# From the fourth chunk on, x is convolved raw in float32 by eight array tiles, and output rows are scaled on GpSimd

## The chip, the cores and the metric

The kernel runs on one core of one Trainium2 chip. The metric is the device time of one launch in microseconds (us): 1162.91 us, the median of three runs from 1162.69 to 1163.97. TensorE is called PE in the profile, VectorE DVE, ScalarE ACT, GpSimd POOL; SP only issues DMAs here. A weight load of PE has rows of its own (PEld).

## The reference

An input x of 8 sequences of 4160 rows and 192 columns is convolved along the sequence: eight heads of 24 columns, seven taps per head, causal (six zero rows ahead of each sequence). The taps are a softmax of a weight table. The result goes, row by row, through a layer with a nonlinearity:

```python
out = np.einsum('hk,bskhg->bshg', w, x_unf)        # convolution: y
...
h = x @ w_in                                       # 192 -> 1024
e = np.exp(h - h_max)
sm = e / (np.sum(e, axis=-1, keepdims=True) + 1e-09)
solu = h * sm
ln = (solu - mu) / np.sqrt(var + 1e-06) * g_ln
return (ln @ w_out).astype(np.float32)             # 1024 -> 192
```

All in float32. The 33280 rows are 260 tiles of 128.

## The kernel before

**Halves.** To use float16 matmuls at float32's accuracy, operands are split: an upper float16 half and a lower one that holds the rest. `y` is written as halves (`upper` on ACT, L313; `lower` on DVE, L322), turned by DMA so that columns lie on partitions (`yT`, and `y2`, a copy of a part on the other 64 partitions), and multiplied with the halves of `w_in` (`whi`, `wlo`).

**One tile of 128 rows.** PE adds up `ph`, 128x1024: `emit_rows` (L736, eight matmuls of 512 columns) and two matmuls with the lower half on 64 array rows (`emit_third`, L759), which are issued in turns for the two halves of the array. DVE scales `ph` and takes its extremum (`emit_max`, L790), ACT makes the exponential (`emit_exp`, L797), DVE multiplies it with `ph` (`emit_mul`, L807), ACT writes the upper half (L815) and the square sums (L819), POOL writes the lower half (`emit_lo`, L827) and SP issues its DMA transpose into `pT`. Five tiles later PE multiplies `pT` with `w_out`'s halves (`emit_out`, L859) into `po`, and DVE empties it into `raw` (`emit_evac`, L869). `raw`'s rows wait until a group of eight tiles has its roots; then each is scaled (`row`, L936 on ACT and L940 on DVE in turns) and stored.

**Three tiles are one step** (`three_steps`), and the order of every engine is written out by hand there. On PE: rows of tile a, a place for convolution, the thirds of a, b and c, rows of b, `po` of an older tile, a second place for convolution, rows of c, two more `po`. `ph` has three pairs of PSUM banks. The two banks left are called singles: `po`, convolution products and small totals take them in turns.

**Chunks.** x is convolved chunk by chunk, one chunk ahead of its use: one chunk of 1024 rows, one of 1056, then 2080 each, 17 in all. A window is 128 rows on partitions, 16 of them overlap, so that it gives 112 rows of `y`. A matmul of `taps` (128 x 112, a band) with windows gives 112 rows of one head. The first three chunks are taken as they are, in float32 (`exact`). From the fourth on, POOL makes halves of x (`halve_steps`, L236, L240, L243), and a head of 9 or 10 windows costs three float16 matmuls (`taps_hi` with `xh`, `taps_hi` with `xl`, `taps_lo` with `xh`); two heads make a group, six matmuls into one single. A chunk has eight groups.

**Scale.** Before a chunk is convolved its magnitude is needed: `sum_squares` takes peaks of quarter pieces on DVE (L181), a small matmul (L95) adds them over the partitions, and a chain of tiny instructions gives the scale `s`.

**What sets the time of such work.** `chores` says at which tile of a chunk its successor's convolutions, turns, copies, loads and peaks are issued; `Queue` lets POOL's halves in piece by piece. Where 2080 rows don't fill tiles, `open` copies up to 96 columns from the chunk before (L339, L340) and mixes two scales (L346, L347).

Of the kernel before, what the change touches and what calls it, by code (L numbers as in the profile page):

```python
# [13 lines left out]
ALU = mybir.AluOpType  # L14
# [5 lines left out]
def kernel(  # L20
# [30 lines left out]

# [9 lines left out]
    spans = []  # L61
    for b in range(B):
        cuts = [0, S // 2, S] if b else [0, FIRST, S // 2, S]
        spans += [(b, t, z - t) for t, z in zip(cuts, cuts[1:])]
    NCH = len(spans)
    NWM = max(-(-n // CW) for _, _, n in spans)
# [55 lines left out]

    class Chunk:
        def __init__(self, ch):
# [7 lines left out]
            self.y16 = {}  # L132
            self.raw = [None] * self.np
            self.sums, self.scaled = 0, False
            self.exact = ch < 3
            self.peaks = 2 * self.np if ch < 2 else self.np if ch < 4 else 0
            self.part = None

        def load(self, j):
# [3 lines left out]
            t = xp.tile(  # L143
                [P, PW, D], F32, name=f"xr_{self.ch}_{j}", tag="xr", bufs=XR
            )
# [67 lines left out]
        def square_peaks(self):  # L213

            if self.peaks < 2 * self.np:
                q = self.part[:, self.peaks : 2 * self.np]
                act.activation(q, q, AF.Square, scale=16.0)

        def add_up(self, bank=None):
            self.tp = total(self.part[:, 0 : 2 * self.np], f"x{self.ch}", bank)  # L220

        def halve_steps(self, j, quick=False):

            if j == 0:
                both = xp.tile([P, 2, NWM, D], F16, name=f"xs_{self.ch}", tag="xs", bufs=2)
                self.xh, self.xl = both[:, 0], both[:, 1]
            a, z = self.cuts[j], self.cuts[j + 1]
            r, h = self.raw[j][:, 0 : z - a, :], self.xh[:, a:z, :]
            xl = self.xl[:, a:z, :]
            size = (z - a) * D * 1e-3  # L230

            def upper():
                if quick:
                    act.activation(h, r, AF.Copy, scale=self.s)
                else:
                    pool.tensor_scalar(h, r, self.s, 1.0, ALU.mult, ALU.mult)  # L236

            return [
                (0.0 if quick else 1.1 * size + 0.2, upper),
                (1.1 * size + 0.2, lambda: pool.tensor_scalar(  # L240
# [1357 lines left out]
```

## Time and profile before

| | |
|---|---|
| median of three runs | 1162.91 us |
| span of the profiled execution, as the page gives it | 1161.5 us |
| PE busy | 1132.2 us, 97% |
| DVE busy | 1016.8 us, 88% |
| ACT busy | 998.0 us, 86% |
| POOL busy | 878.6 us, 76% |
| moved by DMA | 226.95 MB |
| read from HBM, written to HBM | 33.00 MB, 25.56 MB |

The page gives busy time by engine and the costliest groups of instructions. A group's line has the line of the kernel, engine, operation, output and inputs, shape and count, then busy time and the mean length of one in ns, then the engine's idle time just ahead of it and what ended that. The profiled execution is told by its span alone; it lies 1.4 us, 0.1%, under the median of the runs. A matmul's row is longer than its share of the engine, because matmuls overlap: what one costs is the distance from its start to the next one's.

### The profile page before, as it was taken

Reading aid. Unit: us, or ns where it says so; the run is one execution under the profiler, and the core shown is the slowest. Engines: PE = TensorE matmul, PEld = TensorE weight load, DVE = VectorE, ACT = ScalarE, POOL = GpSimd, SP = SyncE. Lnnn points to the kernel's source line nnn. Section 1 sums busy time; section 2 is a strip of 40 time slices with the busy share of each in tenths; the row PEclk is TensorE's granted clock in tenths of the full one; section 3 lists DMA queues with packets and bytes.
Section 4 is the critical chain, followed back from the end, with each engine's and each line's share of the span. In section 5 each row is a group of like instructions: output and inputs, shape, how many; then the busy total and the mean of one; then the engine's idle time right before and its main releaser. Section 6 shows DMA issues by size and latency. Waiting matters only on the chain.

```text
span 1161.5 us, 22374 instructions
## 1 busy us (share of the span) xinstructions
PE 1132.2 (97%) x7742; PEld 692.4 (60%) x7742; DVE 1016.8 (88%) x2058; ACT 998.0 (86%) x1775; POOL 878.6 (76%) x686
## 2 busy tenths in 40 slices
PE   5898999999999999999999999999999999999998
PEld 3575566656666665655656666665666566566556
DVE  8888898988989898998889989888898988788787
ACT  6998988888888888888888888898888889888886
POOL 2745879987888588887868888588788858855665
PEclk9999999999999999999999999999999999999999
DMA  8799899999999999999999999999999998999988
GB/s 226 171 181 180 185 218 205 205 201 202 200 213 195 195 186 220 207 189 199 202 198 190 208 209 199 187 202 208 206 204 198 195 193 170 174 177 186 181 163 188
DMA packets 727391, 226.95 MB, mean 195 GB/s; under 512 B 651614, under 2 KB 725870, under 8 KB 727278
## 3 DMA queue, kind: packets, MB, share of 16 engines
q1 hardware_dynamic: 727278, 225.53, 100.2%
q8 instruction: 60, 0.98, 0.3%
q14 instruction: 53, 0.43, 0.1%
HBM read 33.00 MB, written 25.56 MB: 50 GB/s over the span
## 4 chain that ended last, share of the span: by engine, by line
PE 88%; DVE 5%; ACT 2%; DMA 2%; issue 2%; POOL 1%; SPq 0%; DVEq 0%; ACTq 0%; POOLq 0%
PE po L859 40%; PE ph L736 36%; PE pc L281 6%; PE ph L759 5%; DVE e L807 1%; DMA pT<-p 1%; DVE ph L790 1%; DMA raw_in<-in_moe_w_in_dram 1%; ACT e L797 1%; ACT sq L819 0%; DVE raw L869 0%; DVE y L322 0%; POOL p L827 0%; PE mean L701 0%; DVE wlo L647 0%
## 5 line engine op out<-in xcount | busy, mean ns | idle before, releaser
L827 POOL TENSOR_TENSOR p<-e,p 128x1024 f16<-128x1024 f32 x257 | 548.3, 2138 | 219.5 <-ACT p L815 218.0
L859 PE MATMUL po<-ohl,pT 128*128 128x192 f16 (+1 forms) x4264 | 539.8, 283 | 7.8 <-DVE raw L869 5.4
L859 PEld LDWEIGHTS <-pT 128*128 128x128 f16 x4264 | 384.4, 98 | 167.1 <-issue 7.6
L736 PE MATMUL ph<-whi,yT 128*128 128x512 f16 x1548 | 419.1, 380 | 2.7 <-DVE e L807 2.6
L790 DVE TENSOR_SCALAR_CACHE_REDUCE ph<-ph,cv 128x1024 f32<-128x1024 f32 x248 | 319.1, 1288 | 72.9 <-PE ph L759 56.6
L797 ACT ACTIVATE e<-ph,sm 128x1024 f32<-128x1024 f32 x260 | 289.4, 1113 | 102.0 <-DVE ph L790 95.8
L807 DVE SCALAR_TENSOR_TENSOR e<-ph,cv,e 128x1024 f32<-128x1024 f32 x248 | 317.1, 1279 | 26.0 <-ACT e L797 25.7
L736 PEld LDWEIGHTS <-yT 128*128 128x128 f16 x2064 | 192.6, 98 | 231.3 <-issue 36.3
L815 ACT CAST p<-e 128x1024 f16<-128x1024 f32 x257 | 266.8, 1039 | 27.9 <-DVE e L807 27.3
L819 ACT ACTIVATE sq<-e 128x1024 f32<-128x1024 f32 x260 | 273.4, 1052 | 0.2
L736 PE MATMUL ph<-wlo,yT 128*128 128x512 f16 x516 | 153.5, 379 | 0.0
L869 DVE TENSOR_REDUCE raw<-po 128x192 f32<-128x384 f32 x247 | 136.3, 552 | 14.3 <-PE po L859 13.9
L243 POOL TENSOR_TENSOR xs<-xr,xs 128x960 f16<-128x960 f32 (+1 forms) x56 | 107.6, 1922 | 1.4
L313 ACT ACTIVATE y<-pc 112x432 f16<-112x432 f32 (+5 forms) x140 | 62.8, 469 | 13.8 <-PE pc L281 8.1
L759 PE MATMUL ph<-wlo,yT 64*128 64x512 f16 x269 | 74.0, 380 | 0.0
L322 DVE SCALAR_TENSOR_TENSOR y<-pc,y 112x432 f16<-112x432 f32 (+5 forms) x140 | 72.2, 532 | 0.8 <-ACT y L313 0.8
L281 PE MATMUL pc<-xs,taps_hi 128*112 128x240 f16 (+1 forms) x448 | 72.9, 261 | 0.0
L759 PE MATMUL ph<-wlo,y 64*128 64x512 f16 x251 | 68.6, 380 | 0.0
L181 DVE TENSOR_REDUCE xa<-xr 128x1 f32<-128x384 f32 x112 | 66.6, 617 | 0.0
L281 PEld LDWEIGHTS <-taps_hi 128*112 128x112 f16 x448 | 52.4, 130 | 16.4
L240 POOL TENSOR_SCALAR xr<-xr,s 128x960 f32<-128x960 f32 (+1 forms) x56 | 57.5, 1027 | 2.9
L281 PE MATMUL pc<-xs,taps_lo 128*112 128x240 f16 (+1 forms) x224 | 58.5, 261 | 0.0
(148 smaller groups left out, 787.6 us busy)
## 6 DMA issues: line engine op xcount, KB each, us to landing
out_dram<-raw SPq DMA_DIRECT2D x127, 192.0 KB, 3.0
xr<-in_x_dram SPq DMA_DIRECT2D x41, 480.0 KB, 4.7
xr<-in_x_dram SPq DMA_DIRECT2D x22, 384.0 KB, 4.1
pT<-p SPq DMA_TRANSPOSE x263, 4.6
y<-yT SPq DMA_DIRECT2D x15, 140.0 KB, 3.1
y<-yT SPq DMA_DIRECT2D x15, 126.0 KB, 3.1
yT<-y SPq DMA_TRANSPOSE x102, 3.7
raw_out<-in_moe_w_out_dram SPq DMA_DIRECT2D x1, 1536.0 KB
```

The costliest lines, as they stand in the source:

```text
L243: (2.1 * size + 0.2, lambda: pool.tensor_tensor(xl, r, h, ALU.subtract)),
L281: nc.tensor.matmul(o, tp[:, h + j, :], r, start=q == 0, stop=q == len(ops) - 1)
L736: nc.tensor.matmul(bank, lhs, w[:, r, n * 512 : (n + 1) * 512], start=start and j == 0, stop=stop and j == len(ops) - 1,)
L759: nc.tensor.matmul(banks_of(t)[n], y[q, t.off : t.off + P], wlo[q, 1, n * 512 : (n + 1) * 512], start=start, stop=not start,)
L790: dve.tensor_scalar(t.ph, t.ph, t.cv[:, 0:1], None, ALU.mult, ALU.min, accum_out=t.bias)
L797: act.activation(t.e, t.ph, AF.Exp, bias=t.bias, scale=-1.0, accum_out=grp.z[:, g : g + 1])
L807: dve.scalar_tensor_tensor(t.e, t.ph, t.cv[:, 3:4], t.e, ALU.mult, ALU.mult, accum_out=t.grp.s1[:, t.g : t.g + 1],)
L815: act.copy(t.p16[:, :, 0, :], t.halves)
L819: act.activation(junk, t.e, AF.Square, accum_out=t.grp.s2[:, t.g : t.g + 1])
L827: eng.tensor_tensor(t.p16[:, :, 1, :], t.halves, t.p16[:, :, 0, :], ALU.subtract)
L859: nc.tensor.matmul(t.po[:, 0:n], t.pT[:, a, :], w, start=j == 0, stop=j == len(ops) - 1)
L869: dve.tensor_reduce(t.grp.raw[:, t.g, :], t.po[:, 0 : 2 * D].rearrange("p (a d) -> p d a", a=2), AX.X, ALU.add,)
```

## The change

The first three chunks stay as they are, but the third ends at row 4096 of the second half of the first sequence, and from there on a chunk is a whole number of tiles: twelve of 16 tiles, then two of 18, whatever the sequence borders. Nothing is left over at a chunk's end, so `open`'s copies are gone for them.

From the fourth chunk on (`Strips`) x stays raw. A piece is 48 rows: 16 of overlap and 32 that count. Partitions 0 to 47 hold the pieces of one half, 64 to 111 of the other; two such tiles, `late` 0 and 1, hold the first and second half of a chunk. A matmul takes 64 array rows and 32 array columns, a tile of the array: eight of them, two row halves times four column groups, do one head of a chunk, each with 8 (or 9) pieces of 24 columns. Two heads are one product; it has 384 (or 432) columns in each of the two singles, which are now one PSUM tile `both`. A chunk has four products instead of eight groups, each emptied by one `upper` and one `lower` on all 128 partitions (two each where the columns cross a block). Halves of x, `taps_hi` and `taps_lo` are gone. The result needs the scale `s` as a factor read per partition, where it was a constant.

Peaks are four per chunk, each over 8 or 9 pieces of 192 columns, all on DVE. Output rows are scaled on POOL but for the last ones. Unused partitions are zeroed once (`clear`). `chores` has fixed tiles for it: products at tiles 0, 3, 6 and 9, peaks at 1, 4, 7 and 10. In a step `emit_evac` of the first old tile comes ahead of the product, and `lower` ahead of `emit_max`.

```diff
     singles = 0
+    both = ps.tile([P, F], F32, name="both")
...
-        return ps.tile([P, 512], F32, name=name, tag=f"single{singles % 2}")
+        k = singles % 2 * 512
+        return both[:, k : k + 512]
...
+    class Strips(Chunk):
...
+        def load(self, j):
+            half, late, t = self.place(j)
+            self.raw[j] = t
+            nt, own = self.nt, slice(64 * half, 64 * half + ROWS)
+            first = self.t0 + late * nt * P // 2 + Q * ((half + late) % 2) - HALO
+            nc.sync.dma_start(
+                t[own],
+                bass.AP(
+                    tensor=x.tensor, offset=first * D,
+                    ap=[[D, ROWS], [2 * Q * D, nt], [1, D]],
+                ),
+            )
...
+        def halves(self, j):
+            late, n = j // 2, self.nt // 2
+            return [(2 * late, j, j % 2 * n, (j % 2 + 1) * n)]
+
+        def sum_squares(self, j, col, a, z):
...
+            dve.tensor_reduce(
+                self.part[:, col : col + 1], self.raw[j][:, a:z, :], AX.XY,
+                ALU.max, apply_absolute_value=True,
+            )
...
+        def product(self, h, n, a, z, bank=None):
+            single(f"pc_{self.ch}_{h}a"), single(f"pc_{self.ch}_{h}b")
+            self.bank = both[:, 512:F]
+            m = self.nt // 2
+            pc = both[:, 512 - m * n * HD : 512 + m * n * HD].rearrange(
+                "p (t e) -> p t e", e=n * HD
+            )
+            for j in range(n):
+                for half, c in STRIPS:
+                    late, own = (half + c) % 2, slice(64 * half, 64 * half + ROWS)
...
+                    nc.tensor.matmul(
+                        pc[
+                            Q * c : Q * (c + 1), late * m : (late + 1) * m,
+                            j * HD : (j + 1) * HD,
+                        ],
+                        taps[own, h + j, 64 * half : 64 * half + Q],
+                        raw[:, c // 2, :, (h + j) * HD : (h + j + 1) * HD],
+                        start=j == 0, stop=j == n - 1,
+                    )
...
+    STRIPS = [(0, 0), (1, 1), (0, 2), (1, 3), (0, 1), (1, 0), (0, 3), (1, 2)]
...
+    def clear(k, late):
+        a, z = (0, NTM)
+        pool.memset(strips[k][late][:, a:z, :], 0.0)
...
+            elif eng is pool:
+                pool.tensor_scalar(o, o, u, 1.0, ALU.mult, ALU.mult)
...
+                fixed("conv", [q + late for q in (0, 3, 6, 9)], [(c1, hg) for hg in c1.groups()])
...
+                fixed("peak", (6, 7, 9, 10) if late else (1, 4, 7, 10),
+                    [(c2, h) for j in range(4) for h in c2.halves(j)])
...
-                g.row(j, act if j % 2 else dve)
+                g.row(j, pool if i < NT - 6 else act if j % 2 else dve)
...
         emit_out(done[0])
+        if not start:
+            emit_evac(done[0])
...
-        emit_evac(done[0])
+        if start:
+            emit_evac(done[0])
...
         if not start:
+            lowers(0)
             emit_max(a)
-        lowers(0)
+        else:
+            lowers(0)
...
-        if not start:
-            add(1)
+        for k, h in work.get("peak", []):
+            sum_up(k, h, i + 2)
```

Where a product stands on PE, in a step of the fourth chunk's time or later: first before (`xs` are the halves of x, `pc` the single it goes to, `ph` the tiles' sums), from the second matmul of a group on.

```order
L281 LDWEIGHTS taps_hi
L281 MATMUL pc_0_4_2281<-xs_1740,taps_hi 112x10x24
L281 LDWEIGHTS taps_lo
L281 MATMUL pc_0_4_2281<-xs_1740,taps_lo 112x10x24
L281 LDWEIGHTS taps_hi
L281 MATMUL pc_0_4_2281<-xs_1740,taps_hi 112x10x24
L281 LDWEIGHTS taps_hi
L281 MATMUL pc_0_4_2281<-xs_1740,taps_hi 112x10x24
L281 LDWEIGHTS taps_lo
L281 MATMUL pc_0_4_2281<-xs_1740,taps_lo 112x10x24
L759 LDWEIGHTS yT_1756
L759 MATMUL ph_2272<-wlo,yT_1756 128x512
```

And the same place now, with the waits on semaphores (the lines are those of the changed kernel: L399 the new product, L799 rows, L822 thirds).

```order
L799 MATMUL ph_3012<-whi,yT_2236 128x512
L399 MATMUL both<-xs_412,taps 32x8x24 [waits DVE_49]
L399 MATMUL both<-xs_412,taps 32x8x24 x3
L399 MATMUL both<-xs_413,taps 32x8x24 x4
L399 MATMUL both<-xs_412,taps 32x8x24 x4
L399 MATMUL both<-xs_413,taps 32x8x24 x4
L822 LDWEIGHTS yT_2236
L822 MATMUL ph_3012<-wlo,yT_2236 128x512
```

Sixteen matmuls of 32 x (8 x 24) stand where six of 112 x (10 x 24) stood. The first waits for DVE: for the `emit_evac` of the `po` that PE finished just ahead of these rows. Before, a group waited for the other single, whose `po` was older.

On DVE, a step with two groups of convolution, before: from a tile's maximum to the third tile's multiplication (`y` lines are `lower`, `xa` peaks, the L940 line an output row).

```order
L790 TENSOR_SCALAR ph_3380,sm_3422<-ph_3380,cv_1569 128x1024 [waits DVE_49,PE_49]
L322 SCALAR_TENSOR_TENSOR y_5_10_3295<-pc_10_2_3389,y_5_10_3295 112x9x48 [waits Activation_49]
L790 TENSOR_SCALAR ph_3396,sm_3427<-ph_3396,cv_1569 128x1024 [waits DVE_49,PE_49]
L807 SCALAR_TENSOR_TENSOR e_3425,s_56_3356<-ph_3380,cv_1569,e_3425 128x1024 [waits Activation_49]
L869 TENSOR_REDUCE raw_3248<-po_3438 128x192 [waits PE_49]
L807 SCALAR_TENSOR_TENSOR e_3429,s_56_3356<-ph_3396,cv_1569,e_3429 128x1024 [waits Activation_49]
L790 TENSOR_SCALAR ph_3397,sm_3495<-ph_3397,cv_1569 128x1024 [waits DVE_49,PE_49]
L869 TENSOR_REDUCE raw_3248<-po_3478 128x192 [waits PE_49]
L940 TENSOR_SCALAR raw_2817,t_40_2414<-raw_2817,t_40_2415 128x192
L181 TENSOR_REDUCE xa_3420<-xr_0_2879 128x1
L181 TENSOR_REDUCE xa_3420<-xr_1_3036 128x1 [waits DMAHW0_49]
L807 SCALAR_TENSOR_TENSOR e_3497,s_56_3356<-ph_3397,cv_1569,e_3497 128x1024 [waits Activation_49]
```

And now, a step with a product and a peak, up to the `po` for which the next product waits (L289 is `lower`, L853 the maxima, L870 the multiplications, L932 `emit_evac`, L377 a peak).

```order
L289 SCALAR_TENSOR_TENSOR y_74<-both,s_2537,y_74 128x16x48 [waits Activation_49]
L853 TENSOR_SCALAR ph_3012,sm_3059<-ph_3012,cv_1782 128x1024 [waits DVE_49,PE_49]
L853 TENSOR_SCALAR ph_3037,sm_3063<-ph_3037,cv_1782 128x1024 [waits DVE_49,PE_49]
L870 SCALAR_TENSOR_TENSOR e_3061,s_48_2692<-ph_3012,cv_1782,e_3061 128x1024 [waits Activation_49]
L932 TENSOR_REDUCE raw_3010<-both 128x192 [waits PE_49]
L870 SCALAR_TENSOR_TENSOR e_3065,s_48_2692<-ph_3037,cv_1782,e_3065 128x1024 [waits Activation_49]
L853 TENSOR_SCALAR ph_3038,sm_3123<-ph_3038,cv_1782 128x1024 [waits DVE_49,PE_49]
L932 TENSOR_REDUCE raw_3010<-both 128x192 [waits PE_49]
L377 TENSOR_REDUCE xa_2835<-xr 128x1 [waits DMAHW3_49,DMAHW1_49]
L870 SCALAR_TENSOR_TENSOR e_3125,s_48_2692<-ph_3038,cv_1782,e_3125 128x1024 [waits Activation_49]
L932 TENSOR_REDUCE raw_3010<-both 128x192 [waits PE_49]
```

The `lower` now stands ahead of the first maximum, the output row is gone, and one long peak stands where two short ones stood.

More of the change, by code (lines that the diff above doesn't have):

```diff
@@ L372 @@
+    chunks = [(Chunk if ch < OLD else Strips)(ch) for ch in range(NCH)]
     w_in, w_out = w_in.bitcast(I32), w_out.bitcast(I32)
@@ L1167, in first_two @@
         emit_hi(u)
-        for c in chunks[3:4]:
-            for j in range(XR - sum(q.np for q in chunks[1:3])):
-                c.load(j)
         wo.value(W, wo.e, pool)
@@ L1321, in three_steps @@
         got = {}
-        def add(n):
-            for c, h in added[n]:
-                sum_up(c, h, i + 2)
         def place(n):
```

259 lines of the change are left out of this document (120 added, 139 removed).

## The prediction

> **What bounds the kernel now.** First the page: who is busy, and what the chain that ended last is made of.
>
> ```profile
> span 1161.5 us, 22374 instructions
> PE 1132.2 (97%) x7742; PEld 692.4 (60%) x7742; DVE 1016.8 (88%) x2058; ACT 998.0 (86%) x1775; POOL 878.6 (76%) x686
> ...
> PE po L859 40%; PE ph L736 36%; PE pc L281 6%; PE ph L759 5%; DVE e L807 1%; DMA pT<-p 1%; DVE ph L790 1%; DMA raw_in<-in_moe_w_in_dram 1%; ACT e L797 1%; ACT sq L819 0%; DVE raw L869 0%; DVE y L322 0%; POOL p L827 0%; PE mean L701 0%; DVE wlo L647 0%
> ```
>
> TensorE sets the end; the convolution (L281) is 6% of it. Then the busy times by stretch, to see where TensorE is short of work:
>
> ```profile
> 60.00:130.00 70.00, 64.49 (x466) 40.92 (x465) 56.50 (x122) 63.18 (x122) 42.88 (x37) 1.00 0.93 180
> 600.00:1100.00 500.00, 500.00 (x3406) 303.10 (x3404) 437.92 (x872) 433.09 (x762) 388.02 (x296) 1.00 1.02 194
> ```
>
> From 600 to 1100 us TensorE (the first busy figure) never idles and its clock is full (1.00); the next engine, VectorE, has 62 us of 500 free. So there a step of three tiles costs the sum of its matmuls. The chain of waits in order of time shows one step (512.79 to 524.72) and the convolution groups around it:
>
> ```profile
> 506.59 0.56 PE pc L281 x6
> ...
> 512.79 1.73 PE ph L736 x8
> 514.52 0.75 PE ph L759 x6
> 515.27 1.83 PE ph L736 x8
> 517.11 1.96 PE po L859 x16
> 519.07 1.73 PE ph L736 x8
> 520.79 3.92 PE po L859 x32
> 524.72 1.73 PE ph L736 x8
> 526.44 0.62 PE pc L281 x6
> ```
>
> A step without convolution is 524.72 - 512.79 = 11.93 us. A group of six float16 matmuls adds 0.62 (240 columns) or 0.56 us (216); a chunk has four of each.
>
> **TensorE's work, removed and added.** Removed in 14 chunks: 56 groups at 0.62 and 56 at 0.56 us = 66.1 us.
>
> Added: 56 products of 16 float32 matmuls (two heads, eight array tiles each), 192 columns wide in twelve chunks and 216 in two. No row shows an array tile of 32 columns, so the price needs bounds. The timeline of TensorE has these neighbours:
>
> ```profile
> 38.88 1.95 PE L701 MATMUL mean<-f_out,even 128*128 128x192 f32 x11
> ...
> 501.79 0.26 PE L281 MATMUL pc<-xs,taps_lo 128*112 128x216 f16 x1
> 501.98 0.39 PE L759 MATMUL ph<-wlo,yT 64*128 64x512 f16 x1
> 501.98 0.39 PE L759 MATMUL ph<-wlo,y 64*128 64x512 f16 x1
> 502.20 0.38 PE L759 MATMUL ph<-wlo,yT 64*128 64x512 f16 x1
> 502.21 0.38 PE L759 MATMUL ph<-wlo,y 64*128 64x512 f16 x1
> ```
>
> A float32 matmul leaves two records (eight matmuls on L701, sixteen records in all). Eleven records take 1.95 us; taking off the last one's 0.33 us leaves ten spacings of 0.162 us for 192 columns. The two 64-row halves of L759 start together (both at 501.98, both again at 502.2): two row tiles run at once at full rate. If eight tiles do the same, a head takes two records, and a product 4 x 0.162 = 0.65 us. If only the two row halves overlap, four times that, 2.6 us; if nothing overlaps, 32 x 0.162 = 5.2 us. I take the overlap of all eight, since the one kind of tiling that this trace has overlaps fully. To the 0.65 I add 0.06 for starting sixteen tiles (some 4 ns each, the shift between 502.20 and 502.21), and 0.10 for one more change of the array's division: L759 starts 0.19 us after the last L281 record, whose own 216 columns take 0.09 (0.56 / 6). Before, a step changed into 64-row tiles and back; now it changes into 64x32 as well. That is 0.81 us, and 0.89 with 216 columns: 48 x 0.81 + 8 x 0.89 = 46.0 us. TensorE alone gains 66.1 - 46.0 = 20.1 us.
>
> **The new wait.** A product's sums now lie in both of the banks that the output products (`po`) use in turn. So the first matmul of a product waits for VectorE to have emptied the `po` just before it (L869, L932 after), and this stands last in VectorE's step: behind the maximum and the multiplication of the third tile and, new, behind a peak (L377) four times as long as a half was. After the product ScalarE and then VectorE empty it, and only then come VectorE's two maxima, since the lower half now stands ahead of them. This closes a round through three engines that no step of the kernel before has, and its length has to be set against TensorE's 11.93 + 0.81 = 12.74 us. The rows for it, from the timelines of VectorE and ScalarE:
>
> ```profile
> 515.13 1.28 DVE L790 TENSOR_SCALAR_CACHE_REDUCE ph<-ph,cv 128x1024 f32<-128x1024 f32 x1
> ...
> 517.15 1.29 DVE L790 TENSOR_SCALAR_CACHE_REDUCE ph<-ph,cv 128x1024 f32<-128x1024 f32 x1 [0.68 <-PE ph L736]
> ...
> 518.36 1.28 DVE L807 SCALAR_TENSOR_TENSOR e<-ph,cv,e 128x1024 f32<-128x1024 f32 x1
> ...
> 519.56 0.55 DVE L869 TENSOR_REDUCE raw<-po 128x192 f32<-128x384 f32 x1
> 520.03 1.28 DVE L807 SCALAR_TENSOR_TENSOR e<-ph,cv,e 128x1024 f32<-128x1024 f32 x1
> ...
> 521.23 1.29 DVE L790 TENSOR_SCALAR_CACHE_REDUCE ph<-ph,cv 128x1024 f32<-128x1024 f32 x1
> ...
> 523.60 1.01 DVE L181 TENSOR_REDUCE xa<-xr 128x1 f32<-128x384 f32 x2
> 524.52 0.40 DVE L940 TENSOR_SCALAR_CACHE_REDUCE raw<-raw,t 128x192 f32<-128x192 f32 x1
> ...
> 516.57 1.11 ACT L797 ACTIVATE e<-ph,sm 128x1024 f32<-128x1024 f32 x1 [0.34 <-DVE ph L790]
> 517.58 0.19 ACT L797 ACTIVATION_READ_ACCUMULATOR e<-ph,sm 128x1 f32 x1
> ```
>
> From start to start VectorE spends 1.21 us on a maximum, 1.20 on a multiplication (L807), 0.47 on emptying `po`, 0.46 on a peak of 384. From a maximum's start to the end of its exponential is 517.77 - 515.13 = 2.64, with a handoff of 0.03 (below) 2.67. The handoffs, from a float32 product of an early chunk and from one wait of `po`, and the sizes that the new pieces are scaled from:
>
> ```profile
> 60.48 1.00 PE L281 MATMUL pc<-xr,taps 128*112 128x120 f32 x8
> ...
> 61.52 0.66 ACT L313 ACTIVATE y<-pc,s 112x480 f16<-112x480 f32 x1
> ...
> 62.22 0.72 DVE L322 SCALAR_TENSOR_TENSOR y<-pc,s,y 112x480 f16<-112x480 f32 x1 [1.03 <-ACT y L313]
> ...
> 91.36 0.55 DVE L869 TENSOR_REDUCE raw<-po 128x192 f32<-128x384 f32 x1
> ...
> 91.97 1.30 PE L859 MATMUL po<-ohl,pT 128*128 128x384 f16 x9 [1.80 <-DVE raw L869]
> ...
> L181 DVE TENSOR_REDUCE xa<-xr 128x1 f32<-128x384 f32 x71 | 38.0, 543 | 0.0
> ...
> L181 DVE TENSOR_REDUCE xa<-xr 128x1 f32<-128x576 f32 x41 | 30.6, 745 | 0.0
> ...
> L313 ACT ACTIVATE y<-pc,s 112x160 f16<-112x160 f32 x5 | 2.0, 392 | 0.3 <-PE pc L281 0.3
> ```
>
> A peak goes from 384 to 1536 elements: (745 - 543) / 192 = 1.05 ns each, 0.46 + 1152 x 1.05 ns = 1.67 us. The upper half goes to 768 elements: (660 - 392) / 320 = 0.84 ns each, 0.66 + 288 x 0.84 ns = 0.90. The lower half: 0.72 + 0.30 = 1.02, less some 0.09 by which the next one starts early, 0.93. The round: `po` emptied to first matmul 0.06 (91.91 to 91.97) + 0.08 for the weights ahead of it; the product 0.65 + 0.06 + 0.16 for the last record's tail; 0.04 (61.48 to 61.52), upper 0.90, 0.03 (62.18 to 62.22); lower 0.93; maximum to multiplication 2.67; then multiplication 1.20, `po` 0.47, multiplication 1.20, maximum 1.21, `po` 0.47, peak 1.67, multiplication 1.20, `po` to its end 0.55. Sum 13.55 us, that is 0.81 more than TensorE's 12.74. The product's own length stands in both, so the difference hardly hangs on it; without a peak the round is 11.9 and costs nothing.
>
> How often: convolutions stand on tiles 0, 3, 6, 9 of a chunk, peaks on 1, 4, 7, 10. Where a chunk's first tile is first or second in its step, three products of four have a peak between them and the one before; where it is third, two. With 16 tiles per chunk the three cases take turns: 2.67 on average, over the 13 chunks in whose time a later chunk's peaks are taken, 35 waits. 35 x 0.81 = 28 us. Bounds: 0.6 to 1.0 each if the extrapolated pieces are off by 0.2, 21 to 35 us.
>
> **What costs nothing.** GpSimd loses the halves (L236, L240, L243) and the copies at chunk borders and gets 240 rows; ScalarE and VectorE lose 120 rows each, and the halves of `y` come in 94 instructions instead of 164. None of these engines sets a step, and all get lighter, so I count no gain; the row work on GpSimd stands behind halves that TensorE reads five tiles later. If that cover went, a row of 192 at 0.84 ns and some 0.26 us (0.42) per tile would be late, 100 us of GpSimd time beside 283 us that it has free. x is read with 16 rows of overlap per 32 instead of per 112: 14 chunks from 26 to 33 MB, 3% of 226 MB moved; the transposes are the same number, and loads come a chunk ahead. Start: the four zeroings on GpSimd and four long peaks of the fourth chunk (6.7 us instead of 2.4) fall where TensorE idled 5.5 us of 70, while ScalarE loses its squares there; I put it at 0, with -5 to +5.
>
> **The sum.** 1161.5 - 66.1 + 46.0 + 28 = 1169.4 us of span. The median of the runs stands 1.4 over this profile's span, so 1170.8; I say 1170.
>
> **Rivals.** *Round hidden (faster).* If VectorE's round fits into 12.74 us the 28 us fall away: 1162.9 - 20.1 = 1143. For it: TensorE never waited from 600 to 1100 us. Against: that stretch has no such round, and 0.81 us is many times the spread of the durations above. It needs the extrapolated upper, lower, peak and product to be a fifth shorter together. *Tiles in order (much slower).* A matmul's two records go to the same tile one after the other. If a record may not start before the one ahead of it in the program, only the second record of one tile and the first of the next overlap: 16 x 0.162 + 0.16 + 0.10 = 2.85 us a product, 2.04 more, 56 x 2.04 = 114 us: 1284. L759 takes its halves in turn, so no row here tells the two apart; but they do run two at a time. *Weights one after another (slower).* A float32 weight load of 112 columns lets the next follow after some 0.1 us (the spacing of L281's eight records, 1.00 us less 0.27, by seven); for 32 columns 0.03. Sixteen per head in a row are 0.43 us against 0.32: 0.2 more a product, 12 us: 1182.
>
> [...]
>
> **How the numbers follow.** Forecast, eight tiles overlap and the round binds: 0.45, own range 1161 to 1181 (the bounds of wait and start, and -3 to +5 on the product). Round hidden: 0.32, 1138 to 1148. Weights one after another: 0.13, 1180 to 1195. In order: 0.10, 1284. The range 1139 to 1198 leaves out the last and a little of the others. A measurement of this kernel tells 0.2%, 2.3 us, from no change: faster is the second case and 0.05 of the first, 0.37; within 0.2%, 0.07; slower, 0.56.
>
> **What would show it.** The profile after should have L399 taking 0.7 to 0.9 us per product, idle time of TensorE ahead of it, put down to VectorE's L932, some 35 times 0.8 us; steps of 13.5 us where a product and a peak meet and of 11.9 where none stands; L377 at 1.75 us, 56 of them. No idle time ahead of L399 makes the second case; a product of 2.8 us the third. The forecast is wrong altogether if TensorE waits at another place, say for `pT` or for weights of the next chunk's `yT`.

## The result and the profile after

The changed kernel takes 1431.9 us, the median of four runs from 1429.72 to 1433.29, against 1163.44 us for the kernel before beside it: 1.23 times as long, with a 95% interval from 1.2282 to 1.2319. The forecast was 1170.

The page of the changed kernel: span, busy time of TensorE and of its neighbours, and the granted clock in 40 slices.

```profile
span 1431.6 us, 23903 instructions
PE 1175.8 (82%) x8854; PEld 667.4 (47%) x8854; DVE 987.7 (69%) x1666; ACT 950.3 (66%) x1543; POOL 768.6 (54%) x751
PEclk8989898999989899898989989799898989999999
```

TensorE is idle for 1431.6 - 1175.8 = 255.8 us, where it was idle for 1161.5 - 1132.2 = 29.3. And although its work shrank it is busy for 1175.8 us; the forecast had 1132.2 - 20.1 = 1112.1. So two accounts are open: 63.7 us of busy time too much, and, since the forecast had 29.3 + 28 = 57.3 us of idle time, 198.5 us of idle time too much. Together they are the 262.2 us between this span and the 1169.4 of the forecast. What TensorE waited for, in total, times and longest:

```profile
PE ph L799 <- DMA yT<-y: 74.6, 9, 11.5
PE both L922 <- DVE raw L932: 71.0, 121, 1.1
PE ph L822 <- DMA y<-yT: 49.8, 4, 14.2
PE both L922 <- DVE y L289: 19.3, 5, 8.8
PE both L922 <- DMA pT<-p: 7.7, 4, 5.4
PE both L399 <- DVE raw L932: 4.4, 3, 2.9
```

The wait that the forecast put ahead of the product (L399) is 4.4 us. In its place stand two others. One is small and everywhere: `po` (L922) waits 121 times for VectorE's L932. The other is large and rare: thirteen times, once at each change of chunk, TensorE waits for the new chunk's `yT`, or for its copy on the other 64 partitions, 74.6 + 49.8 = 124.4 us in all. Twelve of these waits take 6.5 to 14.2 us, the last one 2.3.

The small wait, in a step with a product and a peak, from the timelines of TensorE and VectorE:

```profile
510.28 0.88 PE L399 MATMUL both<-xs,taps 48*32 48x192 f32 x32
511.10 0.39 PE L822 MATMUL ph<-wlo,yT 64*128 64x512 f16 x1
...
517.30 0.55 DVE L932 TENSOR_REDUCE raw<-both 128x192 f32<-128x384 f32 x1
517.91 2.12 PE L922 MATMUL both<-ohl,pT 128*128 128x384 f16 x16 [0.47 <-DVE raw L932]
...
520.18 0.55 DVE L932 TENSOR_REDUCE raw<-both 128x192 f32<-128x384 f32 x1
520.78 2.12 PE L922 MATMUL both<-ohl,pT 128*128 128x384 f16 x16 [0.76 <-DVE raw L932]
```

The product itself costs 511.10 - 510.28 = 0.82 us; the forecast said 0.81. But the two `po` shown start only when the `po` just before has been emptied, although that one lies in the other bank. Before, a `po` waited for the one two places back.

The large wait, at one change of chunk, from the timelines of SP's queue and TensorE:

```profile
476.61 1.31 SPq L419 DMA_TRANSPOSE yT<-y  x1
477.96 1.20 SPq L356 DMA_DIRECT2D xr<-in_x_dram  x2
479.92 8.91 SPq L892 DMA_TRANSPOSE pT<-p  x1
488.93 2.16 SPq L419 DMA_TRANSPOSE yT<-y  x1
493.10 1.89 PE L799 MATMUL ph<-whi,yT 128*128 128x512 f16 x4 [9.63 <-DMA yT<-y]
494.92 1.53 PE L399 MATMUL both<-xs,taps 48*32 48x192 f32 x32
```

SP issues two loads of x; the next transpose of `pT` then holds the queue for 8.91 us, where the median is 2.1 us (2.2 in the kernel before); behind it stands the second of the transposes into `yT` that the next chunk's first tile needs. TensorE waits 9.63 us for it. And the product after it takes 1.53 us, not 0.82. The busy time by stretch shows why (start and end, length, busy times of the five engines, and behind them the granted clock):

```profile
493.10:496.00 2.90, 2.90 (x36) 1.09 (x36) 0.00 (x0) 0.00 (x0) 0.00 (x0) 0.50 1.12 217
496.00:499.00 3.00, 3.00 (x26) 0.74 (x11) 1.51 (x2) 2.32 (x5) 0.00 (x0) 0.52 1.08 203
499.00:502.00 3.00, 3.00 (x22) 1.89 (x21) 2.52 (x5) 1.51 (x3) 0.00 (x0) 1.00 0.91 138
```

After the wait TensorE runs at half its clock for some 6 us, and 3 us are lost. Over the whole trace, busy time times what the clock lacks of 1 adds up to some 45 us (1.7 in the kernel before): 29 behind the twelve long waits, and 16 in the first 190 us. So lost clock makes some 44 of the 63.7 us. The rest is, by estimate, no slower work but the way busy time is counted: a matmul's row reaches past the start of the next one, and ahead of a wait this end counts as busy. Sixteen matmuls of `po` take 2.12 us there and 1.96 in unbroken work (the chain in the prediction); 0.16 us at each of the 121 waits of `po` for L932 make 19 us.

### The profile page after: what moved, and what is told of

Same layout as the page of the kernel before. It is cut to its first block, busy times and chain, and to the rows that moved or that the text cites. A ratio compares the mean times of both kernels' runs of the same rounds, so it can differ in the third digit from the quotient of the medians.

```text
span 1431.6 us, 23903 instructions
## 1 busy us (share of the span) xinstructions
PE 1175.8 (82%) x8854; PEld 667.4 (47%) x8854; DVE 987.7 (69%) x1666; ACT 950.3 (66%) x1543; POOL 768.6 (54%) x751
## 4 chain that ended last, share of the span: by engine, by line
PE 33%; DVE 19%; POOL 15%; issue 12%; ACT 8%; DMA 8%; SPq 4%; DVEq 0%; POOLq 0%; ACTq 0%
PE both L922 15%; PE ph L799 13%; POOL p L890 10%; DVE ph L853 8%; DVE e L870 7%; ACT e L860 4%; DMA xs<-in_x_dram 3%; ACT y L280 3%; PE both L399 3%; SPq L892 3%; DMA yT<-y 2%; DVE raw L932 2%; POOL raw L1001 2%; DMA pT<-p 2%; PE ph L822 1%
## 5 line engine op out<-in xcount | busy, mean ns | idle before, releaser
L922 PE MATMUL both<-ohl,pT 128*128 128x192 f16 (+1 forms) x4264 | 568.4, 288 | 103.2 <-DVE raw L932 71.0
L922 PEld LDWEIGHTS <-pT 128*128 128x128 f16 x4264 | 394.6, 100 | 291.5 <-issue 136.5
L799 PE MATMUL ph<-whi,yT 128*128 128x512 f16 x1548 | 433.4, 390 | 78.5 <-DMA yT<-y 74.6
L853 DVE TENSOR_SCALAR_CACHE_REDUCE ph<-ph,cv 128x1024 f32<-128x1024 f32 x259 | 329.5, 1288 | 135.0 <-PE ph L799 100.1
L870 DVE SCALAR_TENSOR_TENSOR e<-ph,cv,e 128x1024 f32<-128x1024 f32 x259 | 331.0, 1278 | 28.3 <-ACT e L860 22.1
L799 PEld LDWEIGHTS <-yT 128*128 128x128 f16 x2064 | 194.7, 100 | 322.2 <-DMA yT<-y 79.0
L289 DVE SCALAR_TENSOR_TENSOR y<-both,s,y 128x768 f16<-128x768 f32 (+10 forms) x85 | 66.8, 805 | 212.8 <-ACT y L280 175.9
L799 PE MATMUL ph<-wlo,yT 128*128 128x512 f16 x516 | 156.3, 385 | 0.0
L932 DVE TENSOR_REDUCE raw<-both 128x192 f32<-128x384 f32 x247 | 136.7, 554 | 26.9 <-PE both L922 20.4
L280 ACT ACTIVATE y<-both,s 128x768 f16<-128x768 f32 (+10 forms) x85 | 60.1, 731 | 134.7 <-PE both L399 112.0
L822 PE MATMUL ph<-wlo,y 64*128 64x512 f16 x251 | 71.6, 390 | 49.8 <-DMA y<-yT 49.8
L1001 POOL TENSOR_SCALAR raw<-raw,t 128x192 f32<-128x192 f32 x240 | 99.8, 429 | 0.0
L822 PE MATMUL ph<-wlo,yT 64*128 64x512 f16 x269 | 75.4, 386 | 0.0
L993 POOL TENSOR_TENSOR t<-t,mhalf 128x8 f32<-128x8 f32 (+2 forms) x33 | 53.6, 1623 | 2.6
L377 DVE TENSOR_REDUCE xa<-xr 128x1 f32<-128x1536 f32 (+1 forms) x28 | 49.5, 1771 | 3.4 <-DMA xr<-in_x_dram 3.4
L860 ACT ACTIVATION_READ_ACCUMULATOR e<-ph,sm 128x1 f32 x260 | 50.1, 193 | 0.0
L377 DVE TENSOR_REDUCE xa<-xs 128x1 f32<-128x1536 f32 (+1 forms) x28 | 49.4, 1771 | 0.0
L882 ACT ACTIVATION_READ_ACCUMULATOR sq<-e 128x1 f32 x260 | 49.2, 189 | 0.0
```

The costliest lines, as they stand in the source:

```text
L280: act.activation(self.at(0, col + e, col + z, a, b), pc[:, :, e:z], AF.Copy, scale=self.scale(),)
L799: nc.tensor.matmul(bank, lhs, w[:, r, n * 512 : (n + 1) * 512], start=start and j == 0, stop=stop and j == len(ops) - 1,)
L822: nc.tensor.matmul(banks_of(t)[n], y[q, t.off : t.off + P], wlo[q, 1, n * 512 : (n + 1) * 512], start=start, stop=not start,)
L853: dve.tensor_scalar(t.ph, t.ph, t.cv[:, 0:1], None, ALU.mult, ALU.min, accum_out=t.bias)
L860: act.activation(t.e, t.ph, AF.Exp, bias=t.bias, scale=-1.0, accum_out=grp.z[:, g : g + 1])
L870: dve.scalar_tensor_tensor(t.e, t.ph, t.cv[:, 3:4], t.e, ALU.mult, ALU.mult, accum_out=t.grp.s1[:, t.g : t.g + 1],)
```

## The experiments

Five runs take one suspect each; five put edits together or take them apart; one puts a single part of the change into the kernel before; one leaves the loads out; two change the loads' shape. Each was run once, only the kernel before with one tile four times; the four runs of the changed kernel lie 3.6 us apart, so single differences of a few us say nothing.

**One tile or two.** First in the changed kernel:

```diff
-    both = ps.tile([P, F], F32, name="both")
...
-        k = singles % 2 * 512
-        return both[:, k : k + 512]
+        return ps.tile([P, 512], F32, name=name, tag=f"single{singles % 2}")
...
-            pc = both[:, 512 - m * n * HD : 512 + m * n * HD].rearrange(
-                "p (t e) -> p t e", e=n * HD
-            )
+            pc = [
+                bank[:, 0 : m * n * HD].rearrange("p (t e) -> p t e", e=n * HD)
+                for bank in banks
+            ]
```

> The two singles are two tiles again, and upper and lower of a product are issued once per bank. Theory (one tile): in the changed kernel each po waits for the emptying of the other bank too, because both banks are one tile; 71 us of TensorE's idle time stand there. Then these waits fall below 10 us, a step with a product goes from 14.0 to 12.8 us and one of the last steps from 12.7 to 11.9, and the time to about 1350 us, or to 1400 if the waits at the chunks' ends (124 us) grow by what TensorE gains. Rival (the round of the prediction binds, whatever the tiles): steps with a product stay at 13.5 us or more, and the time at 1410 to 1430.

Measured: 1370.9 us, 61 less. TensorE's waits in this kernel (L805, L828 and L928 are here the rows, the thirds and `po`):

```profile
PE ph L805 <- DMA yT<-y: 88.4, 11, 12.7
PE ph L828 <- DMA y<-yT: 55.2, 4, 16.6
PE po L928 <- DVE raw L938: 4.0, 4, 2.1
```

The wait of `po` fell from 71.0 to 4.0 us and the last steps of the kernel from 12.73 to 11.92 us. But the waits at the chunks' ends grew from 124.4 to 143.6 us: what came earlier there had only longer to wait for. The time lies between the two numbers expected of this theory; that the tile is the cause is settled by the next run.

This kernel also shows the round of the prediction, since nothing else holds a step in the middle of a chunk. VectorE empties the `po` ahead of three products in a row, with peaks between them, and TensorE's product waits for the second:

```profile
485.03 0.55 DVE L938 TENSOR_REDUCE raw<-po 128x192 f32<-128x384 f32 x1
...
498.46 0.55 DVE L938 TENSOR_REDUCE raw<-po 128x192 f32<-128x384 f32 x1
...
499.07 0.37 PE L398 MATMUL pc_0b<-xs,taps 48*32 48x192 f32 x4 [0.20 <-DVE raw L938]
...
511.53 0.55 DVE L938 TENSOR_REDUCE raw<-po 128x192 f32<-128x384 f32 x1
```

The round is 498.46 - 485.03 = 13.43 and 511.53 - 498.46 = 13.07 us long. The forecast said 13.55, and 12.74 for TensorE. It holds a product between its first matmul and its last: 0.56 us lie between their starts where nothing waits, 1.26 in the product whose second bank starts at 499.07. By the rows of L398, 35 of the 52 products after 220 us are held so, 19 us in all, where the forecast had 35 and 28 us.

Then one part of the change alone, in the kernel before: its two singles become the two halves of one tile, two lines.

```diff
+    both = ps.tile([P, F], F32, name="both")
...
-        return ps.tile([P, 512], F32, name=name, tag=f"single{singles % 2}")
+        k = singles % 2 * 512
+        return both[:, k : k + 512]
```

> One part of the change alone, in the kernel before: the two singles are the two halves of one tile, nothing else. Theory (one tile): every po waits for the emptying of the other bank; the last steps of the kernel go from 11.9 to 12.7 us as they did in the changed kernel, and with some 80 steps and two convolution groups in most of them the time goes up by 40 to 70 us, to 1200 to 1235. Rival (only a product that fills both banks makes po wait): no change, 1163.

Measured: 1405.17 us against 1163.98, a ratio of 1.2078 with an interval from 1.2053 to 1.2104: 241 us, several times the increase that I expected. The waits of TensorE in this kernel (L861 is `po`, L324 `lower`, L871 the emptying of `po`):

```profile
PE both L861 <- DVE y L324: 129.6, 95, 3.5
PE both L861 <- DVE raw L871: 57.8, 82, 2.3
```

Three rows of its timeline, and the stretch of the second with the clock:

```profile
491.81 2.12 PE L861 MATMUL both<-ohl,pT 128*128 128x384 f16 x16 [3.04 <-DVE y L324]
...
603.14 3.79 PE L861 MATMUL both<-ohl,pT 128*128 128x384 f16 x16 [2.19 <-DVE y L324]
...
607.57 2.12 PE L861 MATMUL both<-ohl,pT 128*128 128x384 f16 x16 [0.65 <-DVE raw L871]
```

```profile
603.10:606.90 3.80, 3.76 (x16) 2.26 (x16) 1.24 (x2) 3.01 (x6) 3.57 (x4) 0.55 0.89 190
```

No address is shared, and yet `po` waits 177 times for what VectorE last did in the other bank. I had thought of `po` after `po`; here it waits above all for the `lower` of a convolution group, of which there are eight per chunk. Some of these waits bring the clock down: the sixteen matmuls behind the one of 2.19 us took 3.79 us instead of 2.12. Of 43 waits of 1.8 us or more ahead of sixteen such matmuls, 12 (the shortest 1.95 us) are followed by 3.1 to 3.8 us, the others by 2.12, even one of 3.04 us. So one tile is a cause by itself, and it needs no product.

**The loads on another queue.**

```diff
-            nc.sync.dma_start(
+            act.dma_start(
                 t[own],
```

> Only the queue of x's loads is changed: ScalarE issues them, SP no longer. Theory (SP's queue is held): after two loads of 576 KB the issue of a pT transpose takes 7 us, and the last transposes of yT stand behind it. Then the wait for yT and y2 at the chunks' ends goes from 124 to some 50 us, and the time to about 1340 us. Rival (the transfers themselves are in each other's way on the DMA engines, whoever issues them): transposes land as late as before, 1420 to 1440. Rival (the last transposes are issued too late by GpSimd's lower halves ahead of them): the same, 1420 to 1440.

Measured: 1486.8 us, 55 more than the change. Waits of TensorE:

```profile
PE ph L799 <- DMA yT<-y: 64.6, 13, 6.8
PE both L922 <- DMA pT<-p: 52.8, 17, 10.2
PE ph L822 <- DMA y<-yT: 48.1, 4, 13.1
```

Freed of the loads, SP's queue is no faster: the loads themselves land later (9.1 us in the median, 7.8 before), and a transpose of `pT` now takes up to 16.3 us to land, where it was 14.0. The theory falls as I had put it, and the total lies above all three expectations. What held a transpose here was the load under way, not the place behind it in SP's queue.

**The loads at other tiles**, still on SP, away from the last transposes:

```diff
-                fixed("load", (4, 4, 6, 6) if late else (-1, -1, 1, 3), [(c2, j) for j in range(4)])
-                fixed("peak", (6, 7, 9, 10) if late else (1, 4, 7, 10),
+                fixed("load", (4, 4, 6, 6) if late else (0, 2, 3, 5), [(c2, j) for j in range(4)])
+                fixed("peak", (6, 7, 9, 10) if late else (4, 6, 8, 10),
-            if c3:
-                fixed("load", (13, 14), [(c3, 0), (c3, 1)])
```

> The loads stay on SP but go to tiles 0, 2, 3 and 5 of the chunk before, no longer two of them to tiles 13 and 14 of the one before that, right ahead of the last transposes of yT; peaks go to tiles 4, 6, 8 and 10. Theory (SP's queue is held by the loads): the waits at the chunks' ends go from 124 to below 50 us, and the time to about 1330 us. Rival (the last transposes are late because of their place in the program and of GpSimd): 110 us or more stay, and the time at 1410 to 1440.

Measured: 1397.5 us. The waits for `yT` and its copy fell from 124.4 to 36.4 us, as the theory had it, and the clock rose to a mean of 0.96, but the time fell by 34 us only, because the loads now come too late for the peaks:

```profile
PE both L399 <- DVE raw L932: 39.9, 15, 9.9
PE both L922 <- DMA pT<-p: 28.7, 16, 5.2
...
DVE xa L377 <- DMA xs<-in_x_dram: 20.7, 2, 10.6
```

VectorE stands in a peak that waits for its load, and the product waits for VectorE. So the loads are the cause of the waits at the chunks' ends, and moving them moves the wait.

**The zeroing later.** At the start of a sequence GpSimd zeroes 16 rows of a piece right behind the load's issue. In the changed kernel it waits there for the load to land:

```profile
POOL xs L365 <- DMA xs<-in_x_dram: 70.6, 6, 14.3
```

```diff
-                    pool.memset(t[64 * half : 64 * half + HALO, w, :], 0.0)
+                    zeros.append((t[64 * half : 64 * half + HALO, w, :], 2))
...
+        run_zeros()
         queue.run(3.8 if i < 20 else 2.0)
```

> Only the zeroing of the 16 rows ahead of a sequence is moved: two steps later on GpSimd, when its load has long landed. Theory (GpSimd is held): seven times GpSimd waits 10 to 14 us for a load that was just issued, and six chunk ends behind that have waits of 68 us in all. Then these six fall to a few us each, and the time to some 1360 us. Rival (SP's queue): the six fall only to the level of the other six, 9 us each, and the time to about 1415.

Measured: 1412.4 us. GpSimd's wait is gone. The six chunk ends behind a zeroing fell from 67.8 to 52.6 us, the six others stayed at 53 (54.2 before). The rival was right: the zeroing costs 2.5 us at each border on top of the loads' hold, 20 us in all with the clock.

**The transposes at once.**

```diff
-            move()
+            while moves:
+                move()
```

> One edit to the changed kernel: the transposes into yT are issued all together at the end of their step (tile 10, where the lower halves of the last product are done), no longer one after each tile's pT in the step behind it. Theory (no margin): the last of them reaches SP's queue at the moment at which the next chunk's first tile needs it, so that every hold of the queue (7 us behind two loads, 12 us behind GpSimd's zeroing) is a wait of TensorE. Issued some 8 us earlier and ahead of the loads, they leave 20 to 50 of the 124 us of waiting at the chunks' ends, and the time goes to 1320 to 1360 us. Rival (the array is starved by the DMA traffic whatever the order): 110 us or more stay, 1420 us.

Measured: 1402.9 us. The first kind of wait vanished, and others came:

```profile
PE both L922 <- DMA pT<-p: 54.7, 11, 8.7
PE ph L822 <- DMA y<-yT: 53.8, 4, 15.8
```

The transposes into `yT` are now in time and those of `pT` behind them late, and the wait for the copy of `yT` did not fall (49.8 us before). The missing margin was real, but the hold goes on to the next transpose in the queue; the time lies between the two that were expected.

**The edits together.** Two tiles, zeroing later and transposes at once:

> Three edits together: two tiles for the two singles, the zeroing two steps later, the transposes into yT at once. If the three causes add: the waits of po gone (60 us), those at the chunks' ends below 40 us, and with less idle time the clock nearer to 1: 1230 to 1290 us. If what TensorE gains by the two tiles comes back as longer waits at the chunks' ends, as it did with the tiles alone (124 to 144 us): 1300 us or more.

Measured: 1332.1 us, the second of the two outcomes: `po` waits 66.8 us for `pT`, and 51.0 us go to the copy of `yT`.

Then the products and the transposes behind them a tile earlier (`conv` at 0, 3, 5 and 8, `turn` at 4 and 9, `double` at 7):

> The three edits, and the products at tiles 0, 3, 5 and 8 in place of 0, 3, 6 and 9, the transposes a tile earlier. Theory (margin): 4 us more margin at each chunk's end take what is left of the waits there: 15 to 35 us less than with the three edits alone, 1200 to 1260 us. Rival (what is left are not these waits): the same time within 5 us.

Measured: 1308.6 us. The 51.0 us for the copy fell away and the wait for `pT` rose from 66.8 to 89.2: 24 us less, as the margin theory had it, yet not down to 1260.

Then each load in two halves (`load` gets `parts`, and halves go to tiles 12, 13, 14, 15 and 0, 1, 2, 4; one product of the fourth chunk reads rows of the sixth here, since a half is loaded too early once):

> The four edits, and each load of x cut into two of 288 KB that are issued at eight tiles instead of four. Theory (long loads hold the queue): no pT transpose takes over 5 us to issue, and what is left of the waits for pT and yT goes; 1180 to 1240 us. Rival (the bytes count, not the pieces): the same as without the cut within 5 us, or longer by the eight more issues of 0.6 us per chunk.

Measured: 1286.6 us; the wait for `pT` is 67.4. Better than the rival, far from the theory: halves issued tile after tile still add up, and transposes of `pT` behind three of them take 5.9 us to issue in the median, where 2.1 us is the median without a load ahead.

Then the halves spread over the chunk, and the same with rows on ScalarE and VectorE again:

```diff
+                    fixed("part", (0, 2, 3, 5, 6), [(c2, 1, (1,))] + [
+                        (c2, j, (k,)) for k in (0, 1) for j in (2, 3)
+                    ])
-                fixed("peak", (6, 7, 9, 10) if late else (1, 4, 7, 10),
+                fixed("peak", (6, 7, 9, 10) if late else (3, 6, 9, 12),
+                fixed("part", (13, 14, 15) if late else (12, 13, 15), [
+                    (c3, 0, (0,)), (c3, 1, (0,)), (c3, 0, (1,))
+                ])
```

> Two tiles, zeroing later, transposes at once, products at 0, 3, 5 and 8, and the halves of the loads now spread: three to tiles 12, 13 and 15, five to 0, 2, 3, 5 and 6 of the next chunk, peaks at 3, 6, 9 and 12; none of them right ahead of the transposes into yT. Theory (every pair of loads holds the transposes behind it for 5 to 9 us): the waits for pT fall from 67 to below 25 us and 48 tiles take 205 us as in the kernel before, where they took 224 with the halves in a row; 1190 to 1220 us. Rival (the loads as a whole are too many for the queue): 48 tiles stay at 220 us or more, 1265 to 1290.

> The same with the output rows on ScalarE and VectorE in turns, as in the kernel before. If GpSimd's rows hold its lower halves and so the transposes: 5 to 20 us less than with the spread loads alone. If they stand beside other work: the same within 3 us, or longer by a few us where VectorE's round is longer by the rows.

Measured: 1261.8 us and, with the rows back, 1259.7. Spreading takes 25 us, but the waits for `pT` are still 52.0 us and 48 tiles take 221 us, not 205. The rows make no difference that single runs can show: GpSimd's work is hidden, as the prediction had it.

**No loads at all** from the sixth chunk on, in the kernel with the spread loads (`load` returns ahead of its DMAs and of the zeroing behind them):

> The kernel with the spread loads, but from the sixth chunk on x is not loaded at all: products and peaks read what the chunk two before left in the same tile, so the output from there on is not the reference's. All other instructions stay. Theory (the loads, slow to land with 48 rows, hold the transposes, and these hold po): without them the waits for pT (52 us) fall below 15 us, and 48 tiles go from 221 to some 205 us, the whole to 1180 to 1200 us. Rival (what is left is VectorE's round and SP's other work): 48 tiles stay above 215 us, 1230 or more.

Measured: 1214.6 us, 47 less. The wait for `pT` falls to 17.4 us, and 48 tiles take 209 to 214 us. The loads hold what I said they hold, but the whole lies above the 1200 of the theory. What is left can be read from this trace. The round stays: 39 of the 50 products after 220 us are held between their first matmul and their last, 28 us in all, and the profile puts every wait there down to VectorE's emptying of `po`. The exponential of tile 35 starts at 222.0 us, 26 us later than in the kernel before (195.7). Behind the start, 10 us are waits for `pT`. With the 20 us that TensorE gains, 1163 - 20 + 28 + 26 + 10 makes an estimated 1207 us, 8 short of the measured time.

**The loads' shape.** What stayed open was whether the loads hold the transposes because they are larger or because they are narrower. Two runs keep places and number and change 16 pieces on 48 partitions into 6 windows on 128, first in the changed kernel. The bytes stay too, but for the last two chunks, whose eight loads shrink from 648 to 576 KB.

```diff
+            m = nt * ROWS // P
             nc.sync.dma_start(
-                t[own],
+                t[:, half * m : (half + 1) * m],
                 bass.AP(
                     tensor=x.tensor, offset=first * D,
-                    ap=[[D, ROWS], [2 * Q * D, nt], [1, D]],
+                    ap=[[D, P], [P * D, m], [1, D]],
                 ),
```

> The changed kernel, each load of 16 pieces on 48 partitions (576 KB) replaced by one of 6 windows on 128 partitions (576 KB too) into the same tile: bytes, places and number stay, only the shape differs, and x lands in the wrong rows from the fourth chunk on, so the output is not the reference's. Theory (48 partitions make a load slow to land): a load alone lands after some 5.5 us in place of 7.2, two in 8 in place of 10, the transposes behind them are held shorter, and the waits at the chunks' ends go from 124 us to 60 to 90, the time to 1350 to 1390. Rival (the bytes make it, whatever the shape): landing times and the total stay within 1%.

> The same replacement in the kernel with the spread, halved loads (3 windows on 128 partitions for 8 pieces on 48, 288 KB each; rows wrong in the same way). Theory (shape): a load lands after some 3.5 us in place of 5.6, the waits for pT fall from 52 us towards the 17 that were left without any loads, and the time from 1262 to between 1220 and 1240. Rival (bytes): 1255 to 1268.

Measured: 1379.7 us (52 less than the change) and 1235.4 us (26 less than the spread loads). The loads by the pages of five kernels (count, size of one, median time to landing): before, the change, the change with 128 partitions, the spread halves, and these with 128 partitions.

```profile
xr<-in_x_dram SPq DMA_DIRECT2D x41, 480.0 KB, 4.7
```

```profile
xs<-in_x_dram SPq DMA_DIRECT2D x24, 576.0 KB, 7.7
```

```profile
xs<-in_x_dram SPq DMA_DIRECT2D x28, 576.0 KB, 5.2
```

```profile
xr<-in_x_dram SPq DMA_DIRECT2D x49, 288.0 KB, 5.5
```

```profile
xr<-in_x_dram SPq DMA_DIRECT2D x57, 288.0 KB, 3.8
```

The same change of chunk as above, with 128 partitions, from SP's queue and TensorE, and the waits of this kernel:

```profile
459.68 1.33 SPq L357 DMA_DIRECT2D xr<-in_x_dram  x2
462.09 3.66 SPq L893 DMA_TRANSPOSE pT<-p  x1
470.02 1.89 PE L800 MATMUL ph<-whi,yT 128*128 128x512 f16 x4 [4.38 <-DMA yT<-y]
```

```profile
PE ph L800 <- DMA yT<-y: 45.4, 9, 9.2
PE ph L823 <- DMA y<-yT: 36.8, 4, 12.5
```

The same 576 KB land in 5.2 us on 128 partitions and in 7.7 on 48; a load of 288 KB on 48 partitions (5.5) takes longer than one of 480 KB on 128 (4.7). The transpose of `pT` behind two loads takes 3.66 us here instead of 8.91 (medians of twelve such cases: 3.3 and 6.8). So the shape makes the loads slow and the hold long; windows are also read from rows that follow each other, pieces with gaps between them, and no run separates this from the partitions. With the shape the waits at the chunks' ends fall from 124.4 to 82.2 us and those for `pT` from 52.0 to 36.2. What loads of this shape still cost in the last kernel, 1235.4 - 1214.6 = 21 us, no run divides into bytes and number.

None of these kernels beats the kernel before; the best one that computes the whole result takes 1259.7 us.

## Why the prediction was wrong, point by point

**TensorE's work: right.** A product takes 0.82 us (forecast 0.81): the eight array tiles run side by side, and the rivals of 2.85 us a product or of serial weights fall.

The timeline has 32 records for a product, two for each of its matmuls; at 0.82 us the second record of one tile did not hold the first of the next, as the 2.85 us supposed.

**The round: right in mechanism, hidden in the changed kernel, its price too high.** Its pieces came out as scaled:

```profile
L377 DVE TENSOR_REDUCE xa<-xr 128x1 f32<-128x1536 f32 x24 | 41.7, 1743 | 3.4 <-DMA xr<-in_x_dram 3.4
L289 DVE SCALAR_TENSOR_TENSOR y<-both,s,y 128x768 f16<-128x768 f32 x36 | 36.6, 1018 | 147.6 <-ACT y L280 117.0 <-DMA yT<-y 27.7 <-DMA xs<-in_x_dram 3.0
L280 ACT ACTIVATE y<-both,s 128x768 f16<-128x768 f32 x36 | 32.4, 901 | 93.0 <-PE both L399 81.7 <-DMA yT<-y 9.7 <-DMA xs<-in_x_dram 1.5
```

A peak is 1.74 us (1.75), a lower half 1.02 (1.02), an upper half 0.90 (0.90). With two tiles the two rounds shown are 13.07 and 13.43 us, 0.33 and 0.69 over TensorE's 12.74, where I had 0.81; the sum over that run is 19 us instead of 28. The 0.08 us for weights in the round were my estimate, and the timeline with two tiles does not show them: 0.06 us lie between the end of `po`'s emptying (498.46 + 0.55) and the matmul at 499.07. The 28 us of the run without loads belong to another order of products, at tiles 0, 3, 5 and 8, and agree with the forecast only by chance. In the changed kernel itself it is not seen as I said: there `po` waits first, ahead of the product, and the step is 14.0 us.

**The step that failed first: "the new wait".** "A product's sums now lie in both of the banks that the output products use in turn", it says, and stops there. I read `both` as two banks that take turns, as before, and priced only the product's need for both. The single tile makes `po` wait for the other bank too. I had seen in the order of instructions that the product waits for the `po` just ahead of it, and took that for the product's need of two banks, without asking the same of `po`. 71.0 us of idle time here, 61 us of time when it alone is undone, 241 us when it alone is done to the kernel before.

**The step that failed worst: "What costs nothing".** There I counted x's loads by their bytes, "3% of 226 MB", and the transposes by their number, "the same". Both are true and neither decides. A load on 48 partitions lands in 7.7 us instead of 5.2, a transpose of `pT` behind two of them holds SP for 8.91 us in the case above, and the last transposes into `yT` come up to that moment without margin, because a product covers all tiles of a chunk for two heads: nothing of the new chunk is whole before its last product, where the kernel before had the first half of the windows done half a chunk earlier. That was to be read from the code: four transposes that start after tile 10, one after each `pT`, while the next chunk's first tile follows the last of 16 at once. My last sentence named `pT` and `yT` as the place where the forecast would be wrong altogether, with no price and no rival of its own.

**A term that was missing: the clock.** I kept it at 1.00. Behind waits of 2.19 and 9.63 us it stood near half for some 4 and 6 us in the two cases shown, and lost clock put some 44 us of busy time on top of the idle time.

The length of a wait alone does not tell what follows: the clock was 0.50 and 0.52 behind 9.63 us in the changed kernel and 0.55 behind 2.19 us in the kernel before with one tile, and there the sixteen matmuls behind a wait of 3.04 us took the usual 2.12 us.

**What cost nothing: half right.** The rows on GpSimd are hidden (1259.7 without, 1261.8 with them, one run each). The start was not: the exponential of tile 35 starts at 257.3 us instead of 195.7. Of these 61.6 us, 11.55 are the first change of chunk, 26.4 the waits of `po` for `lower` (19.3) and for `pT` (7.1), and some 16 more lost clock. No run took the start apart, and what sets it stays open: even without loads from the sixth chunk on, 26 us of it remain. I had priced it at 0.

## What to carry to other kernels

Ask of a merged buffer what else used to take turns in it: here dependencies went by tile, and two banks under one name were one buffer for everyone (177 waits of `po` and 241 us in the kernel before). Price a transfer by its shape and by what stands behind it in time, not by its bytes alone (576 KB landed in 7.7 us in one shape and in 5.2 in another), and when work is put together into fewer and larger pieces, ask when the first piece that the consumer needs is whole. In a kernel whose bound engine is 97% busy, a long wait can cost more than its length: behind the 9.63 us shown, some 6 us at 0.50 and 0.52 of the clock cost TensorE another 3.

## What the runs showed of the hardware that I had not expected

DMA transposes were held by loads under way, whoever issued them: with the loads on ScalarE's queue `pT` took up to 16.3 us to land, with them on SP's 14.0, in the kernel before 8.1. A load of 16 pieces on 48 partitions took half as long again as one of 6 windows with the same bytes on 128 (7.7 and 5.2 us; 5.5 and 3.8 for half the pieces and windows). And behind 2.19 us without a matmul TensorE's clock was 0.55 for the next 3.8 us, where it had been 1.00 in the 3.1 us up to their start, while 3.04 us at another place did not slow the matmuls behind.
